# Splitting all of w_in within the last expert by ScalarE and VectorE, and converting two chunks of w_out there

## The chip, the cores and the metric

The kernel runs on one core of a Trainium2 chip. The metric is the device time of one execution in microseconds. The engines are called as the profile calls them: PE (TensorE matmul), PEld (TensorE weight load), DVE (VectorE), ACT (ScalarE), POOL (GpSimd) and SP (SyncE, which issues most transfers).

## The reference

Chunked softmax attention (4 batches, 8 heads, 576 positions of 64, in chunks of 64) gives x, 2304 x 512. A top-1 mixture of 8 experts follows, and then a dense layer, which is where the change acts:

```python
h = np.maximum(np.einsum('ecd,edf->ecf', disp, w1), 0.0)      # 8 experts, w1 512 x 1024
y = np.einsum('ecf,efd->ecd', h, w2)                          # w2 1024 x 512
out[i] = gate_w[i] * y[expert_idx[i], pos[i]]                 # for each kept token
...
h = x @ w_in                                                  # w_in 512 x 2048
g = h * (1.0 / (1.0 + np.exp(-h)))
return (g @ w_out).astype(np.float32)                         # w_out 2048 x 512
```

The inputs w_in and w_out are float64. The kernel gets them as pairs of 32-bit integers.

## The kernel before

**Tiles and stages.** Attention runs first, then the experts one after the other (`for e in range(E)`), each in tiles of 128 tokens, then the dense layer (called FFN here), in blocks of up to 512 tokens. How many tiles an expert has is known only on the chip: the first tile is always done, further ones stand in nested `tc.If(n_e > 128 j)` (`more`), and what background work was planned for the tiles that don't come is done in the `Else`. In this run expert 6 has three tiles and expert 7, the last, has two.

**An expert's tile** (`moe_tile`): the first layer's matmuls (mh, L845) in two halves, each evicted by ScalarE (hh, L850) and VectorE (hl, L851), then the second layer's (myp, L866), then the norm of the rows by ScalarE (L875), a scale by VectorE (L102 to L104), the f16 pair of the result by ScalarE (L877) and VectorE (L879), and a scatter to y_d by GpSimd (L882). Background work is popped at five places of a tile: ahead of the matmuls, after each half, ahead of the second layer's, and at its sixth step. `slots` is the list of the first tile, `arms[1]` and `arms[2]` those of the second and third.

**w_in and w_out** are each 16 chunks of 128 x 512. A chunk goes through four stages.
- Load: SP brings the pairs into one of three staging tiles fs (`f_load`). The load of chunk k + 3 is issued by b3 of chunk k.
- Conversion (`f_conv`): three VectorE operations b1 (L794), b2 (L797) and b3 (L802) make float32 of the pairs, and a Square on ScalarE (L808) with its accumulator gives the chunk's norm.
- Scale: when all 16 norms of a matrix are there, `f_red` sums them (PE, L124) and `f_sc` makes the scale fs (VectorE, L723 and L102 to L104).
- Split into f16 high and low parts: `f_hi` (L729 f., GpSimd here) and `f_lo` (L732 f., VectorE L734). The source of chunk c lies in slot c + 1 of win or wot, and the result goes to slot c:

```python
def f_hi(m, c, eng=nc.gpsimd):
    eng.tensor_scalar(halves(m, c)[:, 0, :], (win, wot)[m][:, c + 1, :], fs[:, m:m + 1], 1.0, ALU.mult, ALU.mult)
```

Two chunks of w_in are converted in each of the experts 0 to 5, chunks 12 to 14 in expert 6 and chunk 15 in expert 7 (`conv_of`). In the last place of expert 7's first tile stand f_red(0), f_sc(0) and `f_split` of chunks 0 to 3, wholly on GpSimd (L749 to L751). Chunk 4's hi and the chunks 5 to 15 are left to the FFN.

**Between experts and FFN.** `y0_load` (SP) brings the first four tiles of y_d back and transposes them. `y0_fac`, in the first tile of the last expert, behind the background work of the last place, makes their row factors: four VectorE operations (m_dg, L968), eight PE matmuls (L970), a VectorE copy (L971).

**The FFN.** A step s is a pair (block b, column chunk f). `l1` has 12 matmuls into one of three PSUM tiles fh (L1115), then VectorE's th (L1121), ScalarE's sigmoid (L1122), one entry of the background list `bg`, VectorE's g (L1126), ScalarE's f16 cast gh (L1128) and GpSimd's gl (L1130). `l2` of a step (L1143) follows LAG = 29 steps later. The row factors of the next block are made at its steps 4 and 8 (y_dg on GpSimd; y_fac: PE L1103, copy L1104).

The list `bg` is planned by a budget: each step adds 1.5; f_lo with the next chunk's f_hi takes 0.7 of it while there are such chunks; b1, b2, b3 cost 0.4, 0.7 and 0.7, and go into the step while they fit. That makes 25 steps, the first 12 with a split. Behind them come f_red of w_out (`late_sum`), a step with nothing, f_sc with the first hi of w_out, and the splits of w_out, two chunks per step at first and then one.

Of the kernel before, what the change touches and what calls it, by code (L numbers as in the profile page):

```python
# [12 lines left out]
ACTF = mybir.ActivationFunctionType  # L13
# [9 lines left out]
def attention_moe_ffn_kernel(  # L23
# [705 lines left out]
    def f_hi(m, c, eng=nc.gpsimd):  # L729
        eng.tensor_scalar(halves(m, c)[:, 0, :], (win, wot)[m][:, c + 1, :], fs[:, m:m + 1], 1.0, ALU.mult, ALU.mult)  # L730
# [11 lines left out]
    def f_split(m, c, eng=nc.gpsimd):  # L742
        if eng is nc.vector:
            f_hi(m, c, eng)
            f_lo(m, c, eng)
            return
        d = (win, wot)[m][:, c + 1, :]
        o = halves(m, c)
        nc.gpsimd.tensor_scalar(d, d, fs[:, m:m + 1], 1.0, ALU.mult, ALU.mult)  # L749
        nc.gpsimd.tensor_scalar(o[:, 0, :], d, 1.0, 1.0, ALU.mult, ALU.mult)  # L750
        nc.gpsimd.tensor_tensor(out=o[:, 1, :], in0=d, in1=o[:, 0, :], op=ALU.subtract)  # L751
# [226 lines left out]
    NSP = 4  # L978
    conv_of = [[2 * e, 2 * e + 1] for e in range(E - 2)] + [[2 * E - 4, 2 * E - 3, 2 * E - 2], [2 * E - 1]]
    m_dg = [st_s[1][3][:, (t + 1) * P:(t + 2) * P] for t in range(4)]  # L980
    for e in range(E):
# [20 lines left out]
        else:  # L1002
            sp = [lambda c=c: f_split(0, c) for c in range(NSP)]
            slots = [[*cb, *cn], [], [], [], [lambda: f_red(0), lambda: f_sc(0), *sp]]
# [23 lines left out]
        if not last:  # L1028
            sqs, red, sc = [], [], []
            if e + 2 < E:  # L1030
                sq, r, c1, _, _ = prep[e + 2, 0]
                sqs, red, sc = [lambda c=c: sq(c) for c in range(4)], [r], [c1]
            arms[0] = [*l2s, *sqs, *red, *cb, *cn, *sc]
            arms[1] = [l2s[0:1], [l2s[1], *sqs[0:2]], [*l2s[2:4], *sqs[2:4], cb[0], cn[0]], [], [*red, *sc]]
            arms[2] = [[], cb[1:2], [*cb[2:], *cn[1:]], [], []]
        else:
            arms[0] = []
# [12 lines left out]
    LAG = 29  # L1050
# [111 lines left out]
    conv = [(op, cost) for c in range(KFF) for op, cost in zip(f_conv(KFF + c), (0.4, 0.7, 0.7, 0.0))]  # L1162
    f_hi(0, NSP)
    left = 0.0
    while conv:
        step, left = [], left + 1.5
        c = NSP + len(bg)
        if c < KFF:
            step.append(lambda c=c: f_lo(0, c))
            if c + 1 < KFF:  # L1170
                step.append(lambda c=c: f_hi(0, c + 1))
            left -= 0.7
# [8 lines left out]

    bg.append(late_sum)
# [72 lines left out]
```

## Time and profile before

| | us |
|---|---|
| three runs | 853.97, 856.37, 857.06 |
| their median | 856.37 |
| the profiled execution | 850.38 |
| its span | 848.6 |
| PE, PEld busy in it | 722.5, 440.5 |
| DVE, ACT, POOL busy in it | 448.1, 333.2, 359.4 |

The trace shows one execution, the profiled one. Its span runs from the first to the last recorded instruction; 1.8 us of the execution lie around it. The last expert's matmuls begin at 409.36 us, the FFN's first g is at 443.55, and the conversion of w_out ends 86 us later. In a line of the timeline the last bracket is the idle time of the engine ahead of the instruction, and what ended it.

### The profile page before, as it was taken

The numbers are of one execution on the slowest core, as the hardware profiler recorded it, in microseconds if no ns is written. First come the engines' busy times: TensorE is split into PE (matmuls) and PEld (weight loads), VectorE is DVE, ScalarE is ACT, GpSimd is POOL, SyncE is SP. The second block draws the span as 40 slices with busy tenths as digits, with TensorE's granted clock in tenths as the row PEclk, the third lists the DMA queues.
The fourth block names the chain that finished last, engine by engine and source line by source line (L and its number), as shares of the span: only waits on it lengthen the run. The fifth ranks groups of instructions, "written<-read, shape, count | busy, mean of one in ns | idle before, by whom it ended". The sixth has DMA issues, their size and how long they took to land.

```text
span 848.6 us, 14692 instructions
## 1 busy us (share of the span) xinstructions
PE 722.5 (85%) x5526; PEld 440.5 (52%) x5526; DVE 448.1 (53%) x920; ACT 333.2 (39%) x615; POOL 359.4 (42%) x355
## 2 busy tenths in 40 slices
PE   4798764998489989569798776999999999999995
PEld 3677654765456756447553333444444444565442
DVE  4365886654794758678339999633322223222000
ACT  5586737443443536442134455322232223223010
POOL 3475632524571737665167535544223223212111
PEclk9797955899699999979899999999999999999999
DMA  7988983992986798895635235020001000001000
GB/s 170 230 231 206 191 239 59 306 273 56 303 246 162 177 235 239 241 237 123 135 72 102 73 125 124 1 51 1 1 37 38 1 1 37 14 1 39 13 37 38
DMA packets 133325, 103.20 MB, mean 122 GB/s; under 512 B 85472, under 2 KB 112096, under 8 KB 133216
## 3 DMA queue, kind: packets, MB, share of 16 engines
q1 hardware_dynamic: 126784, 83.41, 40.2%
q0 software_dynamic: 5760, 18.39, 7.3%
q8 instruction: 60, 0.98, 0.5%
q14 instruction: 49, 0.40, 0.2%
q10 hardware_dynamic: 672, 0.02, 0.0%
HBM read 73.45 MB, written 14.71 MB: 104 GB/s over the span
## 4 chain that ended last, share of the span: by engine, by line
PE 30%; DVE 8%; issue 7%; DMA 4%; POOL 2%; ACT 1%; POOLq 0%; ACTq 0%; DVEq 0%
PE ops L1143 14%; PE fh L1115 14%; DMA out_dram<-ob,yrow 3%; DVE g L1126 2%; DVE th L1121 2%; DVE wot L797 1%; DVE wot L802 1%; PE mh L845 1%; DVE wot L794 1%; DVE win L734 1%; DMA y_d<-yr,tabs 1%; PE myp L866 0%; POOL win L751 0%; POOL win L749 0%; POOL win L750 0%
## 5 line engine op out<-in xcount | busy, mean ns | idle before, releaser
L1143 PE MATMUL ops<-wot,gh 128*128 128x512 f16 x576 | 171.3, 379 | 0.0
L1115 PE MATMUL fh<-yT,win 128*128 128x512 f16 (+1 forms) x768 | 156.9, 355 | 7.0 <-DVE g L1126 7.0
L1130 POOL TENSOR_TENSOR gl<-g,gh 128x512 f16<-128x512 f32 (+1 forms) x80 | 91.9, 1151 | 163.8 <-ACT gh L1128 163.8
L1115 PEld LDWEIGHTS <-win 128*128 128x128 f16 x960 | 94.2, 98 | 118.1 <-issue 26.1
L845 PE MATMUL mh<-mxT,wsp 128*128 128x128 f16 x1920 | 125.6, 233 | 17.7 <-PEq L930 9.4
L845 PEld LDWEIGHTS <-wsp 128*128 128x128 f16 x1920 | 123.5, 106 | 24.1 <-issue 19.9
L1143 PE MATMUL ops<-wot,gl 128*128 128x512 f16 x288 | 109.2, 379 | 0.0
L1121 DVE TENSOR_TENSOR th<-fh,rb 128x512 f32<-128x512 f32 (+1 forms) x64 | 39.8, 622 | 130.7 <-PE fh L1115 130.7
L1122 ACT ACTIVATE th<-th,fi 128x512 f32<-128x512 f32 (+1 forms) x80 | 54.3, 679 | 133.8 <-DVE th L1121 132.9
L175 DVE SCALAR_TENSOR_TENSOR wsp<-st,s,wsp 128x1024 f16<-128x1024 f32 x64 | 99.6, 1591 | 6.0 <-POOL wsp L172 6.0
L866 PE MATMUL myp<-wsp,hh 128*128 128x512 f16 x320 | 96.5, 384 | 0.0
L1143 PEld LDWEIGHTS <-gh 128*128 128x128 f16 x576 | 56.4, 98 | 64.1
L172 POOL TENSOR_SCALAR wsp<-st,s 128x1024 f16<-128x1024 f32 x56 | 75.2, 1359 | 20.0 <-DVE inv L104 11.4
L1128 ACT CAST gh<-g 128x512 f16<-128x512 f32 (+1 forms) x80 | 45.9, 574 | 73.2 <-DVE g L1126 54.3
L157 ACT ACTIVATE junk<-st 128x1024 bf16<-128x1024 f32 x64 | 67.4, 1053 | 16.4 <-DMA st<-in_moe_w_dram 15.3
L1126 DVE TENSOR_TENSOR g<-fh,th 128x512 f32<-128x512 f32 (+1 forms) x80 | 50.7, 634 | 38.8 <-ACT th L1122 32.4
L866 PE MATMUL myp<-wsp,hl 128*128 128x512 f16 x160 | 61.6, 385 | 8.2 <-DVE hl L851 8.0
L819 POOL DMA_INDIRECT xg<-x_d,tabs x34 | 45.4, 1336 | 35.2 <-issue 9.5
L882 POOL DMA_INDIRECT y_d<-yr,tabs x20 | 23.5, 1175 | 79.3 <-DVE yr L879 36.8
L851 DVE SCALAR_TENSOR_TENSOR hl<-mh,hh 128x512 f16<-128x512 f32 x40 | 27.5, 687 | 48.3 <-ACT hh L850 48.3
L1115 PE MATMUL fh<-st,win 128*128 128x512 f16 x192 | 43.5, 379 | 10.6 <-DVE g L1126 9.3
L866 PEld LDWEIGHTS <-hh 128*128 128x128 f16 x320 | 30.7, 101 | 29.8 <-ACT hh L850 0.8
(194 smaller groups left out, 849.8 us busy)
## 6 DMA issues: line engine op xcount, KB each, us to landing
st<-in_moe_w_dram SPq DMA_DIRECT2D x64, 512.0 KB, 6.4
fs<-in_moe_w_in_dram SPq DMA_DIRECT2D x16, 512.0 KB, 7.0
fs<-in_moe_w_out_dram SPq DMA_DIRECT2D x16, 512.0 KB, 3.4
vbd<-in_v_dram SPq DMA_DIRECT2D x72, 64.0 KB, 3.4
x_d<-xr SPq DMA_DIRECT2D x9, 512.0 KB, 6.1
ku<-in_k_dram SPq DMA_DIRECT2D x6, 512.0 KB, 5.7
qu<-in_q_dram SPq DMA_DIRECT2D x6, 512.0 KB, 8.3
ku<-in_k_dram SPq DMA_DIRECT2D x2, 384.0 KB, 4.2
```

The lines of the kernel that those rows point to most:

```text
L157: nc.scalar.activation(out=junk, in_=st[c], func=ACTF.Square, accum_out=n2[:, c:c + 1])
L172: hi_eng.tensor_scalar(sp[c][:, 0, :], st[c], s, 1.0, ALU.mult, ALU.mult)
L175: lo_eng.scalar_tensor_tensor(out=sp[c][:, 1, :], in0=st[c], scalar=s, in1=sp[c][:, 0, :], op0=ALU.mult, op1=ALU.subtract)
L845: nc.tensor.matmul(out=ps[:, f4, :], lhsT=a[c][:, part, f0:f0 + P], rhs=xt[:, rc, :], start=(n == 0), stop=(n == 3 * KD - 1),)
L866: nc.tensor.matmul(out=yp, lhsT=lh[:, f % 4, :], rhs=b[f // 2][:, part, (f % 2) * DM:(f % 2 + 1) * DM], start=(n == 0), stop=(n == 3 * KF1 ...
L1115: nc.tensor.matmul(out=hp[:, 0:n], lhsT=wv[:, part, c, :], rhs=yT_t[b](rc, n), start=(i == 0), stop=(i == 3 * KD - 1),)
L1121: nc.vector.tensor_tensor(out=th[:, 0:n], in0=hp[:, 0:n], in1=rb_t[b][:, 0:n], op=ALU.mult)
L1122: nc.scalar.activation(out=th[:, 0:n], in_=th[:, 0:n], func=ACTF.Sigmoid, scale=fi[:, 0:1])
L1126: nc.vector.tensor_tensor(out=g[:, 0:n], in0=hp[:, 0:n], in1=th[:, 0:n], op=ALU.mult)
L1128: nc.scalar.copy(out=gh[:, 0:n], in_=g[:, 0:n])
L1130: nc.gpsimd.tensor_tensor(out=gl[:, 0:n], in0=g[:, 0:n], in1=gh[:, 0:n], op=ALU.subtract)
L1143: nc.tensor.matmul(out=o_t[b][t], lhsT=lh[:, t * P:(t + 1) * P], rhs=wv[:, part, :], start=(f == 0 and i == 0), stop=(f == KFF - 1 and i = ...
```

## The change

ScalarE takes f_hi instead of GpSimd. All 16 chunks of w_in are split in the last expert, one hi and one lo each: chunks 0 to 3 after the second half of its first tile, where f_red and f_sc now stand too, 4 and 5 in the tile's last place, 6 to 14 in the second tile, and 15, with the conversion of w_out's chunks 0 and 1, in the third tile's list, which runs as the `Else` in this run. To that end chunk 15 of w_in is converted in expert 6. The FFN's list holds the conversions of the 14 other chunks of w_out only, at 1.2 per step, which makes 21 steps; a step with nothing is put ahead of late_sum; LAG is 28.

```diff
--- before.py
+++ after.py
@@ -726,8 +726,10 @@
     def halves(m, c):
         return (win, wot)[m][:, c, :].bitcast(F16).rearrange("p (h f) -> p h f", h=2)
 
-    def f_hi(m, c, eng=nc.gpsimd):
-        eng.tensor_scalar(halves(m, c)[:, 0, :], (win, wot)[m][:, c + 1, :], fs[:, m:m + 1], 1.0, ALU.mult, ALU.mult)
+    def f_hi(m, c):
+        nc.scalar.activation(
+            out=halves(m, c)[:, 0, :], in_=(win, wot)[m][:, c + 1, :], func=ACTF.Copy, scale=fs[:, m:m + 1]
+        )
 
     def f_lo(m, c, eng=nc.vector):
         o = halves(m, c)
@@ -739,16 +741,9 @@
     fs_p = tc_pool("fs", 1, reuse_waits="tile")
     fs_s = [fs_p.tile([P, 512, 2], I32, name=f"fs{i}") for i in range(3)]
 
-    def f_split(m, c, eng=nc.gpsimd):
-        if eng is nc.vector:
-            f_hi(m, c, eng)
-            f_lo(m, c, eng)
-            return
-        d = (win, wot)[m][:, c + 1, :]
-        o = halves(m, c)
-        nc.gpsimd.tensor_scalar(d, d, fs[:, m:m + 1], 1.0, ALU.mult, ALU.mult)
-        nc.gpsimd.tensor_scalar(o[:, 0, :], d, 1.0, 1.0, ALU.mult, ALU.mult)
-        nc.gpsimd.tensor_tensor(out=o[:, 1, :], in0=d, in1=o[:, 0, :], op=ALU.subtract)
+    def f_split(m, c):
+        f_hi(m, c)
+        f_lo(m, c)
 
     fps_s = ExitStack()
     fps_e = fps_s.enter_context(tc.tile_pool(name="fps_e", bufs=1, space=PSUM, reuse_waits="tile"))
@@ -975,8 +970,8 @@
     yr0 = st_s[1][3][:, 0:8].rearrange("p (t w) -> p t w", w=2)
     yT0 = [st_s[1][i].bitcast(F16).rearrange("p (c t) -> p c t", c=KD) for i in range(2)]
     rb0 = st_s[1][2][:, 0:4 * P]
-    NSP = 4
-    conv_of = [[2 * e, 2 * e + 1] for e in range(E - 2)] + [[2 * E - 4, 2 * E - 3, 2 * E - 2], [2 * E - 1]]
+    NC = 2
+    conv_of = [[2 * e, 2 * e + 1] for e in range(E - 2)] + [list(range(2 * E - 4, 2 * E)), list(range(KFF, KFF + NC))]
     m_dg = [st_s[1][3][:, (t + 1) * P:(t + 2) * P] for t in range(4)]
     for e in range(E):
         last = e + 1 == E
@@ -1000,8 +995,9 @@
             slots[3] = [*([g2] if e else []), lambda: g_next(e + 1, 1)]
             slots[4] = [red2, sc2, *[lambda c=c: hi2(c) for c in range(4)]]
         else:
-            sp = [lambda c=c: f_split(0, c) for c in range(NSP)]
-            slots = [[*cb, *cn], [], [], [], [lambda: f_red(0), lambda: f_sc(0), *sp]]
+            sp = [lambda c=c: f_split(0, c) for c in range(KFF)]
+            slots[2] = [lambda: f_red(0), lambda: f_sc(0), *sp[0:4]]
+            slots[4] = sp[4:6]
 
         def nxt0(k):
             if k < 0:
@@ -1032,9 +1028,11 @@
                 sqs, red, sc = [lambda c=c: sq(c) for c in range(4)], [r], [c1]
             arms[0] = [*l2s, *sqs, *red, *cb, *cn, *sc]
             arms[1] = [l2s[0:1], [l2s[1], *sqs[0:2]], [*l2s[2:4], *sqs[2:4], cb[0], cn[0]], [], [*red, *sc]]
-            arms[2] = [[], cb[1:2], [*cb[2:], *cn[1:]], [], []]
+            arms[2] = [[], cb[1:2], [*cb[2:3], *cn[1:2]], [], [*cb[3:], *cn[2:]]]
         else:
-            arms[0] = []
+            arms[1] = [sp[6:8], sp[8:9], sp[9:13], [], sp[13:15]]
+            arms[2] = [[], sp[15:], [*cb, *cn], [], []]
+            arms[0] = [*sp[6:], *cb, *cn]
         more(e, 1, arms)
         if e + 2 == E:
             t_dma(E - 1, 1)
@@ -1047,7 +1045,7 @@
     right.close()
 
 
-    LAG = 29
+    LAG = 28
     ffn = ExitStack()
     f_pool = lambda name, bufs, **kw: ffn.enter_context(tc.tile_pool(name=name, bufs=bufs, reuse_waits="tile", **kw))
     yr_p = f_pool("yrf", 5)
@@ -1159,17 +1157,10 @@
 
     NB = len(blocks)
     bg = []
-    conv = [(op, cost) for c in range(KFF) for op, cost in zip(f_conv(KFF + c), (0.4, 0.7, 0.7, 0.0))]
-    f_hi(0, NSP)
+    conv = [(op, cost) for c in range(NC, KFF) for op, cost in zip(f_conv(KFF + c), (0.4, 0.7, 0.7, 0.0))]
     left = 0.0
     while conv:
-        step, left = [], left + 1.5
-        c = NSP + len(bg)
-        if c < KFF:
-            step.append(lambda c=c: f_lo(0, c))
-            if c + 1 < KFF:
-                step.append(lambda c=c: f_hi(0, c + 1))
-            left -= 0.7
+        step, left = [], left + 1.2
         while conv and conv[0][1] <= left:
             op, cost = conv.pop(0)
             step.append(op)
@@ -1179,6 +1170,7 @@
         sum_at.append(fps_t.tile([P, 4, P], F32, tag="tp", name="rsum").rearrange("p t f -> p (t f)"))
         f_red(1)
 
+    bg.append(lambda: None)
     bg.append(late_sum)
     bg.append(lambda: None)
     bg.append(lambda: (f_sc(1), nc.vector.tensor_tensor(out=ff, in0=fi[:, 0:1], in1=fi[:, 1:2], op=ALU.mult), f_hi(1, 0)))
```

The order of the instructions changes at three places. In the names, a number behind a tile's name is the number of its buffer; a wait names the semaphore of an engine or of a DMA queue.

VectorE, last expert, first tile, from the last hl to the copy behind y0_fac, before:

```order
L851 SCALAR_TENSOR_TENSOR hl_2156<-mh_2169,hh_2154 128x512 [waits Activation_49]
L826 TENSOR_SCALAR yf_2152<-xg_2146,inv 128x1 [waits DMASW4_49]
L723 TENSOR_REDUCE ft_2121<-fh_2135 128x1 [waits PE_49]
L102 TENSOR_SCALAR fe_2122<-ft_2121 128x1 [waits DVE_49]
L103 TENSOR_SCALAR fs<-fe_2122 128x1 [waits DVE_49]
L104 TENSOR_SCALAR fi<-fe_2122 128x1
L1019 COMPARE_AND_BRANCH
L968 TENSOR_SCALAR st_73<-ident_84,st_73 128x128 [waits DMAHW5_49]
L968 TENSOR_SCALAR st_73<-ident_84,st_73 128x128 x3
L971 COPY st_72<-mh_2168 128x512 [waits PE_49]
```

And now:

```order
L846 SCALAR_TENSOR_TENSOR hl_2156<-mh_2169,hh_2154 128x512 [waits Activation_49]
L821 TENSOR_SCALAR yf_2152<-xg_2146,inv 128x1 [waits DMASW4_49,DVE_49]
L723 TENSOR_REDUCE ft_2121<-fh_2135 128x1 [waits PE_49]
L102 TENSOR_SCALAR fe_2122<-ft_2121 128x1 [waits DVE_49]
L103 TENSOR_SCALAR fs<-fe_2122 128x1 [waits DVE_49]
L104 TENSOR_SCALAR fi<-fe_2122 128x1
L736 SCALAR_TENSOR_TENSOR win<-win,fs 128x512 [waits Activation_49] x6
L1015 COMPARE_AND_BRANCH
L963 TENSOR_SCALAR st_73<-ident_84,st_73 128x128 [waits DMAHW6_49]
L963 TENSOR_SCALAR st_73<-ident_84,st_73 128x128 x3
L966 COPY st_72<-mh_2168 128x512 [waits PE_49]
```

The six f_lo (L736) of chunks 0 to 5 stand ahead of the four operations of y0_fac (L968 before, L963 now), and each waits for ScalarE.

ScalarE in the last expert now, from the second hi of the first tile to the last hi of the second tile (L845 is hh, L870 and L872 evict the second layer):

```order
L730 ACTIVATE win<-win,fs 128x512 [waits DVE_49] x5
L1015 COMPARE_AND_BRANCH
L1015 UNCONDITIONAL_BRANCH x2
L870 ACTIVATE yr_2157,yn_2159<-myp_2172 128x512 [waits DMASW3_49,DMASW5_49,DMASW1_49,PE_49]
L872 ACTIVATE yr_2157<-myp_2172,ys_2161 128x512 [waits DVE_49,Activation_49]
L925 COMPARE_AND_BRANCH
L730 ACTIVATE win<-win,fs 128x512
L730 ACTIVATE win<-win,fs 128x512 [waits DVE_49]
L845 ACTIVATE hh_2153<-mh_2170 128x512 [waits PE_49]
L730 ACTIVATE win<-win,fs 128x512 [waits DVE_49]
L845 ACTIVATE hh_2154<-mh_2171 128x512 [waits PE_49]
L730 ACTIVATE win<-win,fs 128x512 [waits DVE_49] x6
```

Here L730 is f_hi, which ScalarE did not have before; 15 of them now stand between the tiles' evictions, and all but the first of the second tile wait for VectorE.

VectorE in the FFN's second and third step before (L1121 is th, L734 lo, L1126 g):

```order
L1121 TENSOR_TENSOR th<-fh_2136,st_72 128x512 [waits PE_49]
L734 SCALAR_TENSOR_TENSOR win<-win,fs 128x512 [waits Pool_49]
L797 SCALAR_TENSOR_TENSOR wot<-fs_2130,wot 128x512 [waits DVE_49]
L1126 TENSOR_TENSOR g_10045<-fh_2136,th 128x512 [waits Activation_49]
L1121 TENSOR_TENSOR th<-fh_9999,st_72 128x512 [waits DMAHW3_49,DMASW6_49,DMAHW6_49,DMASW0_49,PE_49]
L734 SCALAR_TENSOR_TENSOR win<-win,fs 128x512 [waits Pool_49]
L802 SCALAR_TENSOR_TENSOR wot<-fs_2130,wot 128x512 [waits DVE_49]
L794 TENSOR_SCALAR wot<-fs_2131 128x512
```

And two of the last steps with a conversion now (L789, L792 and L797 are b1, b2 and b3; L1119 is th, L1124 g):

```order
L1119 TENSOR_TENSOR th<-fh_2135,rb 128x512 [waits PE_49]
L789 TENSOR_SCALAR wot<-fs_2129 128x512 [waits DMAHW2_49]
L792 SCALAR_TENSOR_TENSOR wot<-fs_2129,wot 128x512 [waits DVE_49]
L1124 TENSOR_TENSOR g_10557<-fh_2135,th 128x512 [waits Activation_49,Pool_49]
L1119 TENSOR_TENSOR th<-fh_2136,rb 128x512 [waits PE_49]
L797 SCALAR_TENSOR_TENSOR wot<-fs_2129,wot 128x512 [waits DVE_49]
L789 TENSOR_SCALAR wot<-fs_2130 128x512 [waits DMAHW4_49]
L1124 TENSOR_TENSOR g_10584<-fh_2136,th 128x512 [waits Activation_49,Pool_49]
```

Between th and g stood a lo and one or two operations of the conversion; now two operations of the conversion stand there in each step.

## Rows read from the trace of the kernel before

**Rows 1.** Windows: span, busy us of each engine, granted clock PEclk, DMA share, GB/s.

```profile
530.50:534.00 3.50, 3.46 (x10) 1.41 (x11) 1.18 (x2) 1.36 (x3) 1.89 (x2) 0.54 0.02 5
...
560.00:780.00 220.00, 220.00 (x1116) 109.34 (x1114) 64.51 (x115) 62.45 (x105) 63.91 (x70) 1.00 0.05 16
```

**Rows 2.** Chain of waits, FFN: start us, length us, engine, output, line, count.

```profile
530.90 12.05 PE fh L1115 x48
542.96 2.59 PE ops L1143 x12
...
599.94 0.89 PE rps L1103 x8
```

**Rows 3.** Timeline of the FFN's first steps: start us, length us, engine, line, operation.

```profile
476.68 0.68 DVE L1126 TENSOR_TENSOR g<-fh,th 128x512 f32<-128x512 f32 x1
...
480.10 0.68 DVE L1126 TENSOR_TENSOR g<-fh,th 128x512 f32<-128x512 f32 x1
...
504.79 0.68 DVE L1126 TENSOR_TENSOR g<-fh,th 128x512 f32<-128x512 f32 x1
...
506.20 1.48 POOL L1130 TENSOR_TENSOR gl<-g,gh 128x512 f16<-128x512 f32 x1 [2.21 <-ACT gh L1128]
...
506.70 1.53 DVE L802 SCALAR_TENSOR_TENSOR wot<-fs,wot 128x512 int32<-128x512 int32 x1
...
508.15 0.68 DVE L1126 TENSOR_TENSOR g<-fh,th 128x512 f32<-128x512 f32 x1
...
511.98 0.68 DVE L1126 TENSOR_TENSOR g<-fh,th 128x512 f32<-128x512 f32 x1
...
515.08 0.68 DVE L1126 TENSOR_TENSOR g<-fh,th 128x512 f32<-128x512 f32 x1
...
518.96 0.68 DVE L1126 TENSOR_TENSOR g<-fh,th 128x512 f32<-128x512 f32 x1
...
522.06 0.68 DVE L1126 TENSOR_TENSOR g<-fh,th 128x512 f32<-128x512 f32 x1
...
529.12 0.68 DVE L1126 TENSOR_TENSOR g<-fh,th 128x512 f32<-128x512 f32 x1
...
529.72 0.67 DVE L1104 COPY rb<-rps 128x512 f32<-128x512 f32 x1
...
530.54 0.37 PE L124 MATMUL rsum<-fn,ones 128*128 128x16 f32 x2 [4.62 <-ACT gh L1128]
```

**Rows 4.** Timeline of the last expert and the first g of the FFN.

```profile
421.49 0.17 DVE L723 TENSOR_REDUCE ft<-fh 128x1 f32<-128x16 f32 x1 [2.51 <-PE fh L124]
...
422.02 1.22 DVE L968 TENSOR_SCALAR st<-ident,st 128x128 f32<-128x128 f32 x4
...
422.35 1.47 PE L970 MATMUL mh<-st,ones 128*128 128x128 f32 x8 [0.90 <-DVE st L968]
...
425.15 0.60 ACT L875 ACTIVATE yr<-myp 128x512 f16<-128x512 f32 x1 [7.08 <-PE myp L866]
...
426.31 0.69 ACT L877 ACTIVATE yr<-myp,ys 128x512 f16<-128x512 f32 x1 [0.47 <-DVE yinv L104]
...
436.85 0.69 ACT L877 ACTIVATE yr<-myp,ys 128x512 f16<-128x512 f32 x1 [0.47 <-DVE yinv L104]
...
441.50 1.28 ACT L1122 ACT_TABLE_LOAD   x1 [3.96 <-DMA y_d<-yr,tabs]
...
442.32 0.74 DVE L734 SCALAR_TENSOR_TENSOR win<-win,fs 128x512 f16<-128x512 f32 x1
...
442.79 0.72 ACT L1122 ACTIVATE th<-th,fi 128x512 f32<-128x512 f32 x1
...
443.55 0.69 DVE L1126 TENSOR_TENSOR g<-fh,th 128x512 f32<-128x512 f32 x1
```

**Rows 5.** Timeline of VectorE behind the branch that ends expert 6.

```profile
408.27 0.43 DVE L794 TENSOR_SCALAR win<-fs 128x512 int32<-128x512 int32 x1 [0.79 <-DVEq L930]
...
409.46 0.69 DVE L802 SCALAR_TENSOR_TENSOR win<-fs,win 128x512 int32<-128x512 int32 x1
```

## The prediction

> **What bounds the kernel now.** I read the windows first, then the chain of waits, then two timelines. In the window 560:780 PE is busy for all of its 220.00 us at clock 1.00 [rows 1], and the chain of waits from 542.96 on is PE alone, l1 and l2 steps of 2.59 us in turn [rows 2]. So nothing in the tail can be gained by another engine, and whatever moves the instant of the first l2 (L1143, 542.96) moves the end one for one. Ahead of it lies the conversion stretch, 444 to 530, in which PE's 2.59 us are not the step: VectorE is. The distance between two g's (L1126) on VectorE is the step [rows 3]: 3.42 us with f_lo and one conversion operation (476.68 to 480.10), 3.36 with b2 and b3 (504.79 to 508.15), 3.10 with b1 and b2 (511.98 to 515.08), 3.88 with three operations (515.08 to 518.96), 3.10 with b3 and b1 (518.96 to 522.06). One of the operations of a step always meets gl on GpSimd: L802 takes 1.53 at 506.70 while L1130 runs from 506.20 [rows 3]. The stretch ends badly: PE stands 4.62 us in front of f_red (L124, 530.54), which waits for the last norm [rows 3], and the clock is 0.54 in 530.50:534.00 [rows 1], so the four l1 steps from 530.90 take 12.05 where four of 2.59 are 10.36 [rows 2]: 1.69 lost. The third place is the last expert, 418 to 444, where ScalarE, VectorE and PE hand short pieces to each other [rows 4].
>
> **The gain, in the FFN.** Now from the first g (443.55 [rows 4]) to the first l2 (542.96) 99.41 us pass, and 30 l1 steps are done then. The change leaves 14 chunks of three VectorE operations, at 1.2 per step two operations in each of 21 steps, in the cycle (b1,b2), (b3,b1), (b2,b3). All three forms stand in rows 3: 3.10, 3.10 and 3.36, a mean of 3.19. From the first g to the 21st are 20 distances: six cycles of 9.56 and 6.46 for two more, 63.9 with rounding, and one copy of rb (L1104, 0.67 with its overlap 0.6 [rows 3]): 64.5. From the last such g PE starts again as now, 529.12 to 530.90, 1.78. Then six l1 steps at 2.59 up to the first l2, the rps matmuls once (0.89 [rows 2]), and one l1 step, which LAG 28 leaves behind the first l2 and which must be counted for the same work: 19.0. The sum is 85.3. I count no half clock here, because the empty step puts an l1 step ahead of f_red, so that PE stands only about 1.2 us instead of 4.62. **Gain 14.1 us.**
>
> **The price, in the last expert.** The order rows show what is put ahead of y0_fac: six pairs hi (ScalarE) and lo (VectorE). Chunk c+1's source lies in the slot that chunk c's result is written to, so each hi waits for the lo before it and each lo for its own hi: a chain that changes engines twice per chunk. No row of before has a hi on ScalarE. Nearest is the sigmoid with a pointer for scale, same shape, 0.72 at 442.79; the lo is 0.74 at 442.32; the handoff between engines is 0.04 (442.79 + 0.72 to the g at 443.55) [rows 4]. A pair is then 0.72 + 0.74 + 0.06 = 1.52, bounds 1.43 (the 0.69 of L877 at 426.31, and no handoff) and 1.66 (handoffs of 0.1).
> - f_red now comes right behind the first layer's matmuls, so fs follows as soon as VectorE is free: it is idle for 2.51 up to 421.49, so free at 418.98, and the four small operations from L723 to L104 take the 0.53 from 421.49 to L968 at 422.02: some 419.55 with a handoff [rows 4]. Six pairs end at 428.65, where m_dg (L968) began at 422.02: **+6.6**. PE's L970, and behind it in PE's queue the second layer's other half, go with it.
> - PE then stands about 7.5 us instead of 0.90. After 4.62 us the clock was 0.54 [rows 1, 3] and cost 1.69; I take **1.7**, between 0 and twice that.
> - The first tile's evictions (L877 at 426.31 + 0.69) thus end 8.3 later, 435.3. Nine more hi's (chunks 6 to 14) stand on ScalarE ahead of the second tile's L875: eight whole pairs 12.2, the ninth hi 0.7, and 0.2 where the two hh wait; the hl's fall into VectorE's half of the chain. That is 448.4. L875 to the end of L877 is 1.85 (425.15 to 426.31 + 0.69 in the first tile [rows 4]), so 450.3 against 436.85 + 0.69 = 437.54: **+12.8** in all, of which 4.5 is this second chain, because only a part of it finds idle time in the tile.
> - In the Else arm, which this data takes since the last expert has two tiles, stand lo 15 and two conversions. Behind 450.3 come L879 0.8, the branch 0.8 (idle 0.79 at 408.27 [rows 5]), lo 0.74, two conversions of 1.88 (408.27 to 410.15 [rows 5]), the last norm 0.8, the table load 1.28 and the sigmoid 0.72: 8.9, where now 437.54 to 443.55 is 6.0, in which y_d's scatter and the table load (441.50) stand [rows 4]. The scatter now has its 3 us beside the conversions. **+2.9.**
> The first g comes 15.7 us later, with the bounds of pair and clock 13 to 19.
>
> What a table load costs is in the rows: L1122's sigmoid starts at 442.79, 0.01 us after the load's end (441.50 + 1.28) [rows 4], so the load alone is charged. The Trainium skill, ScalarE: Activation LUTs, section What ACT_TABLE_LOAD costs, states a drain of some 1380 ns with each load of some 1283. By that rule the sum, an estimate, would be 1.4 us longer, 859.4; the trace agrees on the load and shows no drain behind it.
>
> **At nothing.** Chunk 15's conversion moves into expert 6's second tile, where VectorE has idle time and PE's idle is its own branch; without that cover 1.9. GpSimd loses the hi's and the four split chunks; it was not late, except that y_d's first scatter may leave sooner. SP gets the load of w_out chunk 18 ahead of y0_load and two more in the Else arm: y0's transposes are wanted at the first l1 only, 15 us off; if a load came late at the first conversion step, 1 us. The splits of w_out keep their count, with hi on ScalarE, three steps earlier, under a PE that is full [rows 1]. The first l1 needs only chunk 0, which is long done.
>
> **Sum.** The profiled execution took 850.38 us with a span of 848.6; 15.7 - 14.1 = +1.6 gives 852.0. The median of the three runs is 856.37, 6.0 above it, so on its basis **858.0 us**: the two halves of the change cancel. A measurement of this kernel can tell about 0.5% (4.3 us) from no change.
>
> **Rivals.**
> *Slower: the two-operation steps do not get faster.* The steps with lo and one conversion take 3.42 [rows 3]; the 3.10 ones are those in which a short b1 stands against gl or the first operation gets through before gl begins. With the hi's gone from GpSimd and from its wait, gl may begin earlier in each step and meet the first operation instead of the second, and both then pay. If all 20 distances are 3.42, the cost is 20 x 0.23 = 4.6: 862.6. It decides from the point at which gl begins before the first operation has ended; for it speaks that gl then holds an operation for its whole 1.48, against it that the three forms of rows 3 from 504.79 on, with no lo and no hi either, are exactly these steps.
> *Faster: the pairs are not a chain.* If a hi need not wait for the lo before it, ScalarE and VectorE work side by side, 0.74 per chunk: y0_fac comes +2.7, the second tile follows PE and not ScalarE, and the first g comes 2.7 + 1.7 + 2.9 = 7.3 later instead of 15.7: 849.6. The order's waits and the slots speak against it; for it only that a wait may be met before its instruction is reached, when ScalarE has other work between.
> *That the change does not do what it says:* it would, if the last expert had one tile, put all the left splits in one run behind it. The first tile's eviction at 426.31 and a second one's at 436.85 [rows 4] show two tiles; I give it nothing.
>
> **Chances.** Forecast 0.66, with an own range of 854 (pairs 1.43, no clock loss) to 863.5 (pairs 1.66, the clock's double, a late load); slower rival 0.20; faster rival 0.14. Of the forecast 0.08 lies over 860.6 and 0.01 under 852.1; of the slower rival 0.04 comes back under 860.6 where another of its terms comes out lower. Faster 0.14 + 0.01 = 0.15, slower 0.16 + 0.08 = 0.24, same 0.61. The range, 852 to 864.5, takes in the slower rival with the spread of its pairs, and leaves out the faster one and the tails, some 0.2.
>
> **What would show it.** Right: in the changed kernel hi and lo alternate on ScalarE and VectorE every 1.5 us with each waiting for the other; L963 (m_dg) near 428.7; the clock under 1 behind it; the first g near 459; g's 3.10, 3.10 and 3.36 apart until 523; an idle of PE before f_red of little over 1 us, a clock of 1.00 there, the first l2 near 542 with one l1 step more to come. Wrong: hi's starting every 0.74; a first g before 454 or after 463; steps of 3.4 all through; a clock that falls again before the first l2; or an l1 that waits for its own chunk or for y0's transposes.

## The result, and the profile after

The changed kernel takes 867.01 us, the median of 5 runs (861.09 to 868.99), against 853.97 us before in the same comparison: a ratio of 1.0131, 95% interval 1.0097 to 1.0166. It is slower by 1.3%, where +0.2% was forecast, and 867 lies over the range's upper end, 864.5. The profiled execution took 861.09 us, with a span of 859.3, 10.7 over the span before. The medians differ by 13.0; the account below is of the 10.7 between the two traces, each of a short execution of its kernel.

The windows of the changed kernel (length, busy us of PE, PEld, DVE, ACT and POOL, granted clock, DMA share, GB/s) show two stretches in which PE does nothing:

```profile
421.00:428.00 7.00, 0.00 (x0) 0.00 (x0) 3.65 (x5) 3.05 (x5) 0.00 (x0) 0.67 0.55 100
428.00:444.00 16.00, 15.50 (x134) 10.70 (x134) 8.70 (x21) 6.64 (x11) 2.47 (x2) 0.83 0.24 57
444.00:460.60 16.60, 0.00 (x0) 0.00 (x0) 7.88 (x17) 6.77 (x12) 1.30 (x1) 0.60 0.27 74
460.60:468.00 7.40, 7.31 (x26) 3.05 (x27) 2.50 (x5) 0.99 (x2) 0.00 (x0) 0.75 0.04 1
468.00:530.00 62.00, 55.65 (x253) 24.65 (x251) 61.59 (x79) 33.84 (x66) 28.61 (x24) 1.00 0.46 128
...
560.00:780.00 220.00, 220.00 (x1096) 107.40 (x1095) 64.40 (x109) 65.62 (x106) 57.27 (x60) 1.00 0.08 18
```

The first, 421 to 428, is the one that the prediction counted. The second, 444 to 460.6, is new: 16.6 us in which VectorE, ScalarE and GpSimd together do 16 us of work and PE none. Behind them the mean granted clock is 0.83 and 0.75. The tail, as in [rows 1], is PE without a gap.

The timeline of the changed kernel, from the chain of splits to the first g and the conversion's end:

```profile
418.90 0.72 ACT L730 ACTIVATE win<-win,fs 128x512 f16<-128x512 f32 x1 [1.46 <-DVE fi L104]
...
419.65 0.75 DVE L736 SCALAR_TENSOR_TENSOR win<-win,fs 128x512 f16<-128x512 f32 x1 [0.79 <-ACT win L730]
...
420.44 0.72 ACT L730 ACTIVATE win<-win,fs 128x512 f16<-128x512 f32 x1 [0.82 <-DVE win L736]
...
428.03 0.87 DVE L963 TENSOR_SCALAR st<-ident,st 128x128 f32<-128x128 f32 x4
...
434.19 0.69 ACT L872 ACTIVATE yr<-myp,ys 128x512 f16<-128x512 f32 x1 [0.47 <-DVE yinv L104]
...
449.17 0.69 ACT L872 ACTIVATE yr<-myp,ys 128x512 f16<-128x512 f32 x1 [0.62 <-DVE yinv L104]
...
449.89 0.75 DVE L874 SCALAR_TENSOR_TENSOR yr<-myp,ys,yr 128x512 f16<-128x512 f32 x1 [0.45 <-ACT yr L872]
450.57 0.75 DVE L736 SCALAR_TENSOR_TENSOR win<-win,fs 128x512 f16<-128x512 f32 x1
...
453.14 2.12 SPq L779 DMA_DIRECT2D fs<-in_moe_w_out_dram  x2
...
455.74 1.28 ACT L1120 ACT_TABLE_LOAD   x1
...
460.59 0.38 SPq L1075 DMA_DIRECT2D yrow<-y_d  x1
...
460.69 15.52 PE L1113 MATMUL fh<-st,win 128*128 128x512 f16 x63 [16.82 <-SPq L1041]
...
465.29 0.69 DVE L1119 TENSOR_TENSOR th<-fh,st 128x512 f32<-128x512 f32 x1 [10.39 <-PE fh L1113]
...
466.96 0.68 DVE L1124 TENSOR_TENSOR g<-fh,th 128x512 f32<-128x512 f32 x1
...
531.60 0.68 DVE L1124 TENSOR_TENSOR g<-fh,th 128x512 f32<-128x512 f32 x1
...
539.61 1.13 PE L1101 MATMUL rps<-dg,ones 128*128 128x128 f32 x8 [1.48 <-DVE ft L723]
```

The rows to compare with [rows 4]: the chain of hi and lo runs at 1.54 us per chunk (418.90 to 420.44), the row factors begin at 428.03, the second tile's L872 ends at 449.86. Then SP issues two loads at 453.14, ScalarE loads its table at 455.74 and is ready at 457.02, and no engine has a row from there until 460.59, when SP has passed its branch (L1041). PE's first l1 starts at that moment: its bracket says 16.82 us idle, released by SP's queue at L1041. In [rows 4] ScalarE had the table at 442.78 and the first g followed at 443.55; PE had by then run its l1 steps ahead. Now l1 comes last, and slowly: 460.69 to 465.29, 4.60 us at a mean granted clock of 0.61, where [rows 2] has 2.59. The first g stands at 466.96.

What fills the time up to 460.59 stands in SP's own instructions at the branch (number, nanoseconds of one, first and last start) and in the windows:

```profile
L1041 SPq EVENT_SEMAPHORE  x8: 17/17/17, 457.1 to 460.3; - x8
```

```profile
458.00:459.00 1.00, 0.00 (x0) 0.00 (x0) 0.00 (x0) 0.00 (x0) 0.00 (x0) 0.50 0.48 193
459.00:460.00 1.00, 0.00 (x0) 0.00 (x0) 0.00 (x0) 0.00 (x0) 0.00 (x0) 0.50 0.03 12
460.00:460.40 0.40, 0.00 (x0) 0.00 (x0) 0.00 (x0) 0.00 (x0) 0.00 (x0) 0.50 0.00 0
```

SP goes through eight semaphore instructions, the last at 460.3. The bytes move at 193 GB/s from 458 to 459 and have come to an end at 460.

The chain of waits at the end:

```profile
540.74 10.36 PE fh L1113 x48
551.10 2.59 PE ops L1141 x12
```

Four l1 steps take 10.36, so the clock is full where [rows 2] has 12.05, and the first l2 stands at 551.10 against 542.96. With the one l1 step that LAG 28 leaves behind it, 8.14 + 2.59 = 10.73: the whole difference of the spans.

### The profile page after: what moved, and what is told of

It is laid out like the page before. It is cut to its first block, busy times and chain, and to the rows that moved or that the text cites. A ratio compares the mean times of both kernels' runs of the same rounds, so it can differ in the third digit from the quotient of the medians.

```text
span 859.3 us, 14698 instructions
## 1 busy us (share of the span) xinstructions
PE 719.1 (84%) x5526; PEld 435.6 (51%) x5526; DVE 448.5 (52%) x924; ACT 354.3 (41%) x647; POOL 326.9 (38%) x315
## 5 line engine op out<-in xcount | busy, mean ns | idle before, releaser
L1113 PE MATMUL fh<-yT,win 128*128 128x512 f16 (+1 forms) x768 | 155.0, 352 | 3.0 <-DVE g L1124 3.0
L840 PE MATMUL mh<-mxT,wsp 128*128 128x128 f16 x1920 | 119.5, 228 | 17.0 <-PEq L925 8.2
L840 PEld LDWEIGHTS <-wsp 128*128 128x128 f16 x1920 | 117.3, 103 | 23.0 <-issue 18.0
L1119 DVE TENSOR_TENSOR th<-fh,rb 128x512 f32<-128x512 f32 (+1 forms) x64 | 39.8, 622 | 131.9 <-PE fh L1113 131.9
L1124 DVE TENSOR_TENSOR g<-fh,th 128x512 f32<-128x512 f32 (+1 forms) x80 | 50.8, 634 | 41.9 <-ACT th L1120 36.8
L1126 ACT CAST gh<-g 128x512 f16<-128x512 f32 (+1 forms) x80 | 46.0, 575 | 60.4 <-DVE g L1124 45.5
```

Of the source, the lines that this page charges most:

```text
L840: nc.tensor.matmul(out=ps[:, f4, :], lhsT=a[c][:, part, f0:f0 + P], rhs=xt[:, rc, :], start=(n == 0), stop=(n == 3 * KD - 1),)
L1113: nc.tensor.matmul(out=hp[:, 0:n], lhsT=wv[:, part, c, :], rhs=yT_t[b](rc, n), start=(i == 0), stop=(i == 3 * KD - 1),)
L1119: nc.vector.tensor_tensor(out=th[:, 0:n], in0=hp[:, 0:n], in1=rb_t[b][:, 0:n], op=ALU.mult)
L1124: nc.vector.tensor_tensor(out=g[:, 0:n], in0=hp[:, 0:n], in1=th[:, 0:n], op=ALU.mult)
```

## The experiments

Theory L, formed from the row at 460.69: the two loads that b3 of w_out's chunks 0 and 1 issues in the last expert's Else arm hold the first l1. SP goes on from the arm to `tc.If(n_e > SPLIT0)`, whose body this data does not run. On the path around the body the program has eight instructions for SP, the eight rows at L1041: each waits until the transfers that SP issued before on one of its eight semaphores have landed, and adds to it the count that the body's own transfers would have added. The first l1 waits for those counts. Theory B: the branch or the Else itself holds l1, not the loads. Theory C: the long idle and its clock are the cost and the wait is not.

One interval serves for comparing traces, because executions of one kernel differ by several us ahead of the last expert (its first matmul lies between 409.20 and 419.06 in the traces of the study): from the last expert's first matmul to the first g ("start"), and from there to the first l2 ("FFN"), both in us.

| kernel | median us | ratio to before | start | FFN |
|---|---|---|---|---|
| before | | 1 | 34.19 | 99.25 |
| the change | 867.01 | 1.0131 (1.0097 to 1.0166) | 55.74 | 83.98 |
| e1, loads later | 857.63 | 1.0016 (0.9987 to 1.0044) | 48.54 | 83.68 |
| e2, before and two loads | 854.55 | 0.9994 (0.9964 to 1.0025) | 33.78 | 99.35 |
| e3, no conversion in the Else | 859.53 | 1.0037 (1.0001 to 1.0074) | 46.63 | 87.79 |
| e4, e1 and half a slot | 847.89 | 0.9923 (0.9882 to 0.9963) | 41.24 | 83.69 |
| e5, e1 and factors first | 854.09 | 0.9976 (0.9941 to 1.0011) | 45.25 | 83.68 |
| e6, e4 and e5 | 846.74 | 0.9908 (0.9869 to 0.9947) | 36.93 | 83.68 |
| e7, before and two late loads | 862.92 | 1.0071 (1.0030 to 1.0112) | 40.70 | 100.50 |
| e8, before and an empty step | 852.96 | 0.9987 (0.9955 to 1.0020) | 33.23 | 95.97 |
| e9, e6, scale sooner | 844.69 | 0.9896 (0.9867 to 0.9925) | 38.13 | 82.48 |
| e10, e6 with LAG 29 | 846.68 | 0.9896 (0.9864 to 0.9928) | 37.77 | 86.28 |
| e11, the change, no branch | 858.82 | 1.0000 (0.9969 to 1.0030) | 48.62 | 83.96 |
| e12, the change and half a slot | 862.18 | 1.0043 (1.0014 to 1.0073) | 48.39 | 83.94 |

In the table FFN ends at the first l2 of the timeline, 0.16 us ahead of the chain's. The kernel before was timed in every comparison anew, with medians of 853.97 to 857.80; a ratio is to its own.

### The loads out of the Else arm (e1)

```diff
-    def f_conv(k):
+    def f_conv(k, load=True):
...
-            f_load(k + 3)
+            if load:
+                f_load(k + 3)
...
-        ops = [f_conv(c) for c in conv_of[e]]
+        ops = [f_conv(c, not last) for c in conv_of[e]]
...
     with tc.If(n_e[E - 1] > SPLIT0):
         y0_load()
         y0_fac()
+    for c in range(NC):
+        f_load(KFF + c + 3)
```

> The changed kernel, with the loads of w_out chunks 19 and 20 issued behind the branch that follows the last expert instead of in the Else arm. Theory L (the loads): SP passes that branch only when every load that it issued has landed, and the first l1 waits for SP; so the first l1 starts within 2 us of the last expert's last matmul (near 444 instead of 460.7), the first g comes near 457.8 (table load 455.74 + 1.28, sigmoid 0.72) instead of 466.96, and the profiled execution loses 9 us, 861.1 to 852; against before +0.2%. Theory B (the branch): the first l1 waits for the end of the Else on all engines, or for the last scatter, whatever SP issues there; the first l1 stays at 455 to 461 and the time within 2 us of 861. Theory C (the clock): PE's long idle and the low clock are the cost and not the wait; the first l1 stays late too.

857.63 us, ratio 1.0016, where the change has 1.0131: the intervals don't meet. The timeline of e1:

```profile
449.46 6.96 PE L1116 MATMUL fh<-st,win 128*128 128x512 f16 x24 [2.34 <-DVE win L736]
...
456.66 2.12 SPq L779 DMA_DIRECT2D fs<-in_moe_w_out_dram  x2
...
458.63 9.62 PE L1116 MATMUL fh<-st,win 128*128 128x512 f16 x36 [2.21 <-DVEq L1042]
...
459.26 1.28 ACT L1123 ACT_TABLE_LOAD   x1
...
460.55 0.72 ACT L1123 ACTIVATE th<-th,fi 128x512 f32<-128x512 f32 x1
...
461.31 0.69 DVE L1127 TENSOR_TENSOR g<-fh,th 128x512 f32<-128x512 f32 x1 [0.28 <-ACT th L1123]
```

The first l1 starts 7 us before the loads leave, waits only for its own chunk's lo, and the first g waits for the sigmoid. (The 2.21 us of a later l1 are a wait for VectorE to reach the same branch.) From the row factors (432.35 here) to the first g it is 28.96 us, in the change 38.93: 10 us, expected 9. Theories B and C fall. The table load is again followed by the sigmoid at once, at 460.55, 0.01 us behind its end. The Trainium skill, ScalarE: Activation LUTs, section What ACT_TABLE_LOAD costs, has a drain of some 1380 ns beside the load for every switch to a different set; neither trace shows it on this path.

### Two loads added to the kernel before (e2, e7)

```diff
         else:
             arms[0] = []
+            arms[2] = [[], [], [lambda: f_load(KFF + 1), lambda: f_load(KFF + 2)], [], []]
```

> The kernel before, with nothing added but the loads of w_out chunks 17 and 18 issued a second time, into the same tiles, in the last expert's Else arm. Theory L: the first l1 starts when the later of them has landed, near 444 instead of 437.0, th can follow only 3 to 4.6 us behind it, so the first g comes near 449 instead of 443.55: 4 to 7 us slower than before, with no change on VectorE, ScalarE or GpSimd. Theory B or C: the first l1 stays near 437 and the time within 1 us of before.

Nothing: 0.9994. Theory L as stated missed. The reason is in the trace of e2, the rows of SP and PE:

```profile
428.22 1.42 SPq L784 DMA_DIRECT2D fs<-in_moe_w_out_dram  x2
...
436.85 17.39 PE L1116 MATMUL fh<-st,win 128*128 128x512 f16 x72 [2.27 <-PEq L1044]
```

And SP's instructions at the branch:

```profile
L1044 SPq EVENT_SEMAPHORE  x8: 17/17/17, 433.5 to 435.2; - x8
```

SP has little to do in the last expert and reads the branch early; nothing made it wait, so the loads left at 428.22, and SP's last semaphore instruction at the branch stands at 435.2, ahead of the first l1. From the end of the second issue (428.22 + 1.42) to it are 5.6 us; in the change they are 5.0 (453.14 + 2.12 to 460.3). It is not the place of a load in the program that costs; what is left is that its issue must wait for a late VectorE operation. e7 adds that wait, 0.33 us of copies:

```diff
+            def again(c):
+                nc.vector.tensor_copy(fe2[:, 1:2], fs_s[(KFF + c) % 3][:, 0, 0:1])
+                f_load(KFF + c)
+
+            arms[2] = [[], [], [lambda: again(1), lambda: again(2)], [], []]
```

> As e2_before_two_loads, but each of the two repeated loads stands behind a VectorE copy of one column of the tile that it overwrites, in the Else arm, so that SP cannot issue it ahead of VectorE's arrival there. Theory L: the loads leave at 439 to 440 and land near 444 to 445, the first l1 waits for SP until then instead of starting at 437, behind 7 us of idle at the low clock, so the first g comes near 450 instead of 443.55 and the time is 6 to 8 us over before. If the loads are innocent: the first l1 near 437 and the time within 1 us of before.

862.92 us, ratio 1.0071, 6.2 us over its own before (856.69). The timeline of e7:

```profile
442.25 0.81 SPq L784 DMA_DIRECT2D fs<-in_moe_w_out_dram  x2
442.44 1.02 POOL L882 DMA_INDIRECT y_d<-yr,tabs  x1 [2.96 <-DVE fe L1040]
...
448.85 1.28 ACT L1128 ACT_TABLE_LOAD   x1 [7.48 <-DMA y_d<-yr,tabs]
...
448.88 13.31 PE L1121 MATMUL fh<-st,win 128*128 128x512 f16 x54 [9.38 <-SPq L1049]
...
454.82 0.68 DVE L1132 TENSOR_TENSOR g<-fh,th 128x512 f32<-128x512 f32 x1
```

The wait of the change on a kernel that has none of its other parts: PE idle for 9.38, released by SP at the branch (L1049), 5.8 us behind the end of the second issue (442.25 + 0.81). SP's last semaphore instruction there stands at 448.7. But PE's wait is not the only one here. The last scatter to y_d, issued at 442.44, landed 6.4 us later, at 448.85, where before it took 2.9 (438.60 to 441.50), and the table load waits for it. By that path alone the first g would stand, by estimate, at 448.85 + 1.28 + 0.72 + 0.04 = 450.9; it stands at 454.82. So SP's wait holds the last 3.9 us by itself, and what comes ahead of them both waits share. In the change the scatter's landing held nothing: the table load at 455.74 follows ScalarE's last norm at once.

### The branch taken out (e11)

```diff
-    with tc.If(n_e[E - 1] > SPLIT0):
-        y0_load()
-        y0_fac()
     moe.close()
```

> The changed kernel without the last branch, tc.If(n_e > SPLIT0) with y0_load and y0_fac, whose path this data never takes (left out: the case of a last expert with over 1792 tokens). The loads of chunks 19 and 20 stay in the Else arm. In the instruction order the first l1 then waits for y0's own transfers alone; before, it waits for the counts that SP adds in the path not taken, behind the landing of all its transfers. If that path is what ties l1 to the loads: the first l1 starts right behind the last expert's tiles, with no wait for SP, and the time is that of e1_loads_later, 857 to 858. If the loads themselves hold l1 back (their queue, the memory, the tile), the first l1 stays behind their landing and the time is that of the change, 867.

858.82 us, ratio 1.0000, as e1. The loads leave late, at 460.51, and the first l1 has long begun:

```profile
452.32 7.93 PE L1110 MATMUL fh<-st,win 128*128 128x512 f16 x36 [0.91 <-ACT win L730]
...
460.51 2.12 SPq L779 DMA_DIRECT2D fs<-in_moe_w_out_dram  x2
...
465.16 0.69 DVE L1121 TENSOR_TENSOR g<-fh,th 128x512 f32<-128x512 f32 x1 [0.28 <-ACT th L1117]
```

So it is neither the queue nor the memory: the path around the branch's body ties l1 to the loads.

### No conversion in the Else (e3)

```diff
-    NC = 2
+    NC = 0
```

> The changed kernel with no w_out chunk converted in the last expert: all 16 in the FFN at 1.2 per step, 24 steps. Theory L: nothing is loaded in the Else, so the first l1 follows the last matmul (near 444), the first g comes near 455.4 (the scatter's landing at 453.9, then th and sigmoid) and three more two-operation steps cost 9.6: 861.1 - 11.6 + 9.6 = 859. Theory B or C: the first l1 stays at 453 or later, the first g near 463, and the time is near 867.

PE's rows of e3 at the conversion's end:

```profile
540.44 0.58 PE L124 MATMUL rsum<-fn,ones 128*128 128x16 f32 x2 [3.09 <-ACT gh L1126]
540.86 10.69 PE L1113 MATMUL fh<-yT,win 128*128 128x512 f16 x36
...
553.78 0.38 PE L1141 MATMUL ops<-wot,gh 128*128 128x512 f16 x1 [2.02 <-DVE wot L736]
```

The mechanism holds (the first l1 is at 452.56 with 1.52 idle behind ScalarE's hi, start 46.63 instead of 55.74), the sum was wrong: 859.53 is 7.5 under the change, not 2. Three more steps with a conversion don't cost 9.6, since the l1 steps are there anyway: by the prediction's 3.19 each costs 0.6 over PE's 2.59. FFN grew by 3.8 in the trace, and what follows it by 2.2 (310.52 against 308.36). Of these 6.0 the steps' excess is 1.8; the rest arises at the conversion's end: PE stands 3.09 in front of f_red, where the change has 0.83, the next three l1 steps take 10.69 instead of 7.8, and the first l2 waits 2.02 for a split of w_out. Once the loads were out of the way, the two conversions in the Else were worth about 2 us (e1 857.63 against e3 859.53), which is not clear of the spread: the intervals meet.

### The chain of hi and lo (e4, e12)

```diff
-    win = reg_p.tile([P, KFF + 1, 512], F32, name="win")
+    win_f = reg_p.tile([P, KFF * 512 + 768], F32, name="win")
+    win = win_f[:, 0:KFF * 512].rearrange("p (c f) -> p c f", f=512)
...
+    def src(m, c):
+        return wot[:, c + 1, :] if m else win_f[:, c * 512 + 768:c * 512 + 1280]
```

f_hi, f_lo and f_conv then use src(m, c). A hi writes the first half of its slot, which is now free.

> As e1_loads_later, and the source of chunk c of w_in lies one and a half slots behind its result instead of one, so that a hi no longer overwrites the source of the lo before it, only that of the one before that. If the slot makes the chain: hi's start every 0.75 us instead of 1.54, the row factors begin near 424 instead of 428.0, PE idles some 3.5 instead of 7.5 us and keeps its clock, the second tile follows PE, and the first g comes 7 to 8 us earlier than in e1_loads_later: some 845, 0.6% faster than before. If the chain is made by something else (handoff, the lo's own wait), hi's stay 1.5 apart and the time stays that of e1_loads_later.

847.89 us, ratio 0.9923: 9.7 under e1, and under the kernel before. The timeline of e4:

```profile
421.97 1.33 ACT L734 ACTIVATE win<-win,fs 128x512 f16<-128x512 f32 x2 [1.46 <-DVE fi L104]
...
422.73 5.04 DVE L740 SCALAR_TENSOR_TENSOR win<-win,fs 128x512 f16<-128x512 f32 x6 [0.79 <-ACT win L734]
...
427.69 0.87 DVE L968 TENSOR_SCALAR st<-ident,st 128x128 f32<-128x128 f32 x4
...
428.03 2.07 PE L970 MATMUL mh<-st,ones 128*128 128x128 f32 x8 [4.12 <-DVE st L968]
```

And the window behind it:

```profile
428.00:431.00 3.00, 2.97 (x11) 2.26 (x12) 1.31 (x5) 0.00 (x0) 0.00 (x0) 0.50 0.51 98
```

Six lo's take 5.04 in place of the 8.46 from 419.65 to 428.11 in the change. So the slots made the chain, as the prediction had it. PE idles 4.12 instead of 7.53, and behind it the granted clock is 0.50 (428 to 431): the clock still falls here, against the expectation. Its eight matmuls of L970 take 2.07, where e5, with no idle ahead of them, has 1.05 at 1.00.

> The changed kernel with the source one and a half slots behind and nothing else; the loads stay in the Else arm. If chain and loads are two costs that add: the chain's 8 to 10 us go and the 9 us of the loads stay, 857 to 859, with the first l1 still waiting for SP for some 10 us and more. If the shorter chain makes the loads leave early enough, they cost nothing any more and the time is that of e4_half_slot, 848.

The first l1 of e12:

```profile
461.04 14.15 PE L1117 MATMUL fh<-st,win 128*128 128x512 f16 x56 [12.92 <-SPq L1045]
```

862.18 us, ratio 1.0043. From e12 to e4 the loads are worth 1.2%, from the change to e1 1.15%; the chain is worth 0.88% from the change to e12 and 0.93% from e1 to e4. The two costs add, and in e12 PE's first l1 still waits for SP, 12.92 us.

### The place of the row factors (e5, e6)

```diff
-            slots[2] = [lambda: f_red(0), lambda: f_sc(0), *sp[0:4]]
-            slots[4] = sp[4:6]
+            slots[2] = [lambda: f_red(0), lambda: f_sc(0)]
...
                 with tc.If(n_e[e] <= SPLIT0):
                     y0_fac()
+                for f in sp[0:6]:
+                    f()
```

> As e1_loads_later, with the six splits of the first tile behind y0_fac instead of ahead of it. The term of the prediction on PE's idle (+6.6 and 1.7 for the clock) says: the row factors begin right behind f_sc (near 419 by the clock of the changed kernel, within 8 us of the tile's first matmul instead of 16.8), PE does not idle for 7.5 us, its clock stays at 1.00, and since the chain of hi and lo on ScalarE now sets the end of the second tile alone, 3 to 4 us are won of the 8.3: some 854. Rival: the chain alone sets the end and the place of y0_fac is worth nothing: the time stays that of e1_loads_later, 857.6, within 1 us.

854.09 us, 3.5 under e1, as expected; the ratios' intervals still meet (0.9976 and 1.0016). The start falls from 48.54 to 45.25. The row factors begin 9.35 behind the first matmul (8 were expected), and PE is busy without a gap there, at a clock of 1.00.

> As e5_fac_first with the source one and a half slots behind. If chain and place are two costs: the last expert's two tiles run at the pace that they had before, the first g comes 2.9 us later than before behind the same first matmul (the Else arm alone), and the FFN's gain of 13 to 14 us stays: some 845, 2 to 3 us under e4_half_slot. If e4_half_slot already freed PE, the time is that of e4_half_slot, 848.

846.74 us, ratio 0.9908. The start is 36.93, 2.74 over before, near the 2.9 of the Else arm that was expected; but that is not a measure of the arm. e10, the same up to the first g, has 37.77, and e8, the kernel before up to there, has 33.23. The arm alone stands between the second tile's eviction by ScalarE and the first g:

```profile
446.12 0.69 ACT L877 ACTIVATE yr<-myp,ys 128x512 f16<-128x512 f32 x1 [0.79 <-DVE yinv L104]
...
454.73 0.69 DVE L1132 TENSOR_TENSOR g<-fh,th 128x512 f32<-128x512 f32 x1 [0.29 <-ACT th L1128]
```

From 446.81 to 454.73 it is 7.92, and 7.91 to 7.93 in e1, e4, e5, e9, e10 and e11, against 6.01 before: the arm costs 1.9. Against e4 the time falls by 1.1, less than the 2 to 3 expected and within the spread.

### The conversion's end (e8, e9, e10)

e8 is the kernel before with one entry added:

```diff
+    bg.append(lambda: None)
     bg.append(late_sum)
```

> The kernel before with one empty entry ahead of late_sum, nothing else. The prediction's reading of the conversion's end says: one more l1 step of 2.59 us stands in PE's queue ahead of f_red and fills part of its 4.62 us idle, and the clock does not fall, so the first l2 comes 2.6 + 1.7 us sooner: 4.3 us, 0.5% faster than before. Rival: f_red's result or the later split then comes late for the first l2, and nothing is won.

Ratio 0.9987, where 0.5% faster was expected: no difference that can be told. The trace shows both readings in part: PE stands 1.31 instead of 4.62 ahead of f_red, the clock is 1.00 in the windows there, FFN falls by 3.3; but then the first l2 waits for its split of w_out:

```profile
545.42 0.38 PE L1143 MATMUL ops<-wot,gh 128*128 128x512 f16 x1 [0.81 <-POOL wot L730]
...
546.62 0.38 PE L1143 MATMUL ops<-wot,gh 128*128 128x512 f16 x1 [0.83 <-DVE wot L734]
```

What follows the first l2 takes 306.78 instead of 305.80: 2.3 of the 4.3 us are left.

e9 drops the empty entry behind late_sum from e6:

```diff
     bg.append(late_sum)
-    bg.append(lambda: None)
```

> As e6_fac_first_half_slot without the empty entry between late_sum and f_sc. The 1.4 us by which the FFN's term was too good are put down to the rps matmuls, which wait 1.47 us in PE's queue for f_sc's reduction to free the PSUM tile that they share. If so, that wait goes, the distance from the first g to the first l2 falls from 83.7 to 82.3 and the time by 1.4 us, to 845. Rival: the wait is for dg on GpSimd or the splits then come early without use: the distance stays within 0.3 us.

FFN is 82.48 instead of 83.68, 1.2 of the expected 1.4, and the rps matmuls follow the l1 without a wait. The time, 844.69, is 2 under e6, within the spread. This version has the lowest median of the study, 1.0% under the kernel before (0.9867 to 0.9925); from e6 and e10 it can't be told apart.

> As e6_fac_first_half_slot with LAG 29 instead of 28. By the prediction's counting LAG moves one l1 step from behind the first l2 to ahead of it: the first l2 comes 2.6 us later, what follows it takes 2.6 us less, and the time stays within 0.5 us of that of e6_fac_first_half_slot. Rival: a wait of the first l2 for its split, hidden by the later start, makes it faster.

FFN is 86.28, 2.60 more, and what follows it 305.84 against 308.39, 2.55 less: LAG only moves an l1 step, as counted.

## Why the prediction was wrong, step by step

The span grew by 10.7 where +1.6 was the sum. Of the 9.1 that were missed 7.7 lie ahead of the first g and 1.4 behind it. One of the prediction's own signs of being wrong came, a first g after 463.

| term | forecast | measured |
|---|---|---|
| a pair hi and lo | 1.52 | 1.54 |
| row factors begin | 428.65 | 428.03 |
| PE's idle there | 7.5 | 7.53 |
| row factors to the first tile's last ACT eviction | 6.65 | 6.85 |
| second tile's ends | 450.3 | 449.86 |
| from there to the first g | 8.9 | 17.10, of which SP's wait 9.2 |
| first g | 459.25 | 466.96 |
| first g to the 21st | 64.5 | 64.64 |
| first g to the first l2 | 82.7 | 84.14 |

- **What failed: "At nothing", on SP's loads.** The prediction put the two loads of the Else arm at nothing, or 1 us where a conversion would wait for its chunk, and said that "the first l1 needs only chunk 0, which is long done". It asked who reads the tiles that are loaded, and not who waits for SP. The path from the arm through the branch held the first l1 back until the loads had landed. Without it the first g stood at 455.74 + 1.28 + 0.72 + 0.04 = 457.8, so the wait cost 9.2: e1 gives back 9.4 us of the median, and e11, which takes away the branch alone, has the time of e1. The prediction's own instruction rows could not show it: the waits that count stand on SP, on the path around a branch's body, which no row of the fences held.
- **The steps that were right.** The chain of the splits was 0.02 per pair off and is made by the slots (e4), and the row factors' delay and its clock cost stood as counted (6.85 us from them to the eviction's end where [rows 4] gives 4.98, +1.9 for a forecast of 1.7). Part of the match at 428 is chance: the last expert's first matmul came 1.9 later than before, and its first layer ran at full clock in 5.53 us where it had taken 8.08.
- **The Else's own term** was 1.0 too large. Without SP's wait the stretch behind the second tile is 457.8 - 449.86 = 7.92 where 8.9 was counted, +1.9 and not +2.9. The branch's 0.8 did not come: the lo starts at 450.57, right behind L874 (449.89 + 0.75). So the wait of 9.2 was in part covered, in the sum, by terms that came out lower.
- **A wrong reading without effect.** Chunk 15's conversion stands in expert 6's third tile, not its second. PE's idle ahead of the last expert was 3.55, before 4.54.
- **The gain in the FFN** was 14.1 forecast and 12.7 measured. The 20 distances were 64.64 for 64.5 (whose six cycles and two add up to 63.8, not 63.9), and the clock stayed at 1.00 in front of f_red with 0.83 idle. The missing 1.4 is the wait of the rps matmuls for f_sc, 1.48 in PE's queue at 539.61: late_sum comes three steps sooner, and f_sc, which frees its PSUM tile, now falls on the step whose row factors take the same tile. e9 takes 1.2 of it away.
- **The rivals.** The slower one (steps of 3.42) did not come: the steps are 3.10 and 3.37. The faster one (no chain) did not come either, until the slots were moved. The kernel was slower, by a mechanism that no rival named.

So the change gives 12.7 in the FFN, pays 14.2 for it in the last expert (457.8 - 443.55), and 9.2 more for two loads. With the loads behind the branch, the half slot, the factors first and f_sc sooner (e9) the kernel is 1.0% faster than before.

## What to carry to other kernels

In a program built like this one, a transfer that is issued in an arm of a branch can hold everything behind the next branch: before a load is put there, look for who waits for the issuing queue behind it, not only for who reads the tile, and issue the load behind the last branch where its own issue must wait for a late operation. Where a pass writes its result into the slot of its neighbour's source, two engines that share the pass take turns; half a slot more made the 1.54 us of a chunk 0.84 here. A stage that fills a bound engine's free time must itself be cheap where it goes: price it by the excess over the step that is there anyway, and look at what a longer stage does at its end, as e3 showed.

## What the runs showed that was not expected

- The same two loads in the same arm cost nothing when they left at 428.22 (e2) and 6.2 us when they left at 442.25 (e7): SP ran ahead of the other engines through the branches and was only as late as the operation that it waited for. In e7 part of the 6.2 is the scatter's late landing.
- PE's first layer in the last expert ran in 5.53 us behind an idle of 3.55, and in the kernel before, behind 4.54, had 8.08 for the same 96 matmuls. The idle alone does not decide it: behind 3.77 us it took 5.53 in e12 and 7.05 in e3.
